# Sixteen weight loads issued from GpSimd's queue instead of SyncE's, in a linear-attention and feed-forward kernel

## The chip, the cores and the metric

One core of a Trainium2 chip runs the whole program. The metric is the device time of one execution in microseconds (us), and the smaller the better. Before the change the median of three runs is 593.93 us (593.01 to 596.69).

The engines are named as in the profile: PE is TensorE (matmuls), PEld its weight loads, DVE is VectorE, ACT is ScalarE, POOL is GpSimd, and SP is SyncE, which computes nothing and here issues transfers. Each engine works through its own instructions in program order and waits where an operand is not ready. A transfer (DMA) is issued by an engine and then carried out by 16 DMA engines, which all issuers share.

## The reference

The input is a linear attention with a decaying complex state, and the result goes through a feed-forward layer. Batch 4, 8 heads, 768 tokens, head size 48; the feed-forward layer goes from 384 to 2048 and back.

```
for t in range(S):                                  # per batch and head
    new_re = ar * S_re - ai * S_im                  # a_t normalised to |a| <= 0.999
    new_im = ar * S_im + ai * S_re
    S_re, S_im = new_re + outer(k_t, v_t), new_im
    y_t = q_t @ S_re
x = y, heads side by side                           # 3072 x 384
h = x @ w_in                                        # 384 x 2048
out = (h * sigmoid(1.702 * h)) @ w_out              # 2048 x 384
```

The two weight matrices are given in 64-bit floating point, everything else in 32-bit.

## The kernel before

The 3072 tokens are cut into 12 units of 256 tokens (`T`), three to a batch element. Each unit u goes through three parts:

- `prepare(u)` loads the decay (`ri`) and the queries and keys (`qk`), computes the running decay magnitude and angle with ACT and DVE (logarithm, exponential and sine tables on ACT; scans on DVE at L582, L598 and L616), and turns the queries and keys by it (L456). POOL writes one-column edges for the scans (L571 and L575, memsets) and makes small copies (L594, L653). Unit 0 is prepared in two halves of 128 tokens so that PE can begin early.
- The turned queries and keys are moved into another layout by `remap`, which copies from SBUF to SBUF in five transfers (L664, L665, L667), once with source `qr` and once with source `qk`. SP issues them. `attend(u)` needs them: PE computes scores (`p_ps`, L702), transposes (`k_ps`, L748), states (`z_ps`, L755) and outputs (`x_ps`, L728).
- `moe(u)` computes the feed-forward layer in eight slices of 256 hidden columns. H is the first matmul (L794, into `h_ps`), then ACT applies Silu (L803 in unit 0, L807 after it), and O is the second (L827, into `o_ps`). Slice i needs the w_in slice A*i* and the w_out slice U*i*. Each H and O has two pieces. Unit 0 runs on whole 32-bit weights, six matmuls to a piece of H and four to a piece of O; the later units run on weights split into a high and a low part.

The sixteen weight slices are loaded once, in the order A0, A1, U0, A2, U1, A3, U2, A4, U3, A5, U4, A6, U5, A7, U6, U7. One load is a 768 KB transfer of 64-bit values into one of four buffers (`raws`), number n into buffer n mod 4. `convert(n)` makes 32-bit values of it: ACT turns the low words in place (L474), and DVE works in three steps (L475, L478, L481), of which the last frees the buffer. So load n can only start once load n - 4 has passed its L481. `split(n)` makes the high part (L494, ACT) and the low part (L499, DVE).

Later in the program SP also issues 48 loads of weights (`raw_w`) and ten of decay values for a check of the value ranges (L849, L872).

The order of all this is not written by hand. Every operation is added to a `Plan` with an engine, an estimated duration, a rank and what it reads and writes. `forward` runs a list scheduler over the operations: each engine starts at the time given for it in `FREE` (POOL at 3.3), takes the ready operation of lowest rank, and a transfer is put on a single line of transfers with estimated costs. `backward` corrects the ranks from the end, `time` rates the result, and the best order of many rounds is emitted; each engine then executes its part in exactly that order, whatever the real times are. A different cost for one kind of operation can therefore change the order of any engine.

The instructions ahead of the plan are emitted first. On POOL these are a few memsets and copies, the last of them the clearing of `qkh` (L397 and L398).

Of the kernel before, what the change touches and what calls it, by code (L numbers as in the profile page):

```python
# [12 lines left out]
I32 = mybir.dt.int32  # L13
# [63 lines left out]

def lag(a, b):
    return LAG if b != "PE" else 0.0 if a == b else LAG_PE


class Plan:
# [31 lines left out]
    def forward(self, rank, stay):  # L114

        ops, after = self.ops, self.after
        left = [len(o[4]) for o in ops]
        ready = [0.0] * len(ops)
        free = dict(FREE)
        wait = {e: [] for e in ENGINES}  # L120
        can = {e: [] for e in ENGINES}
        table, hw, dma, idle = None, 0.0, 0.0, 0.7
        todo, held = self.groups(), None
        clock = Clock()
        kinds, kind = self.kinds, None
        for n, k in enumerate(left):
            if not k:
                heapq.heappush(wait[ops[n][0]], (0.0, n))
        start = [0.0] * len(ops)
        done = 0  # L130
        while done < len(ops):
            best = None
            for e in ENGINES:
                while wait[e] and wait[e][0][0] <= free[e]:
                    n = heapq.heappop(wait[e])[1]
                    heapq.heappush(can[e], (rank[n], n))
                if can[e]:
                    s = free[e]
                elif wait[e]:
                    s = wait[e][0][0]  # L140
                else:
                    continue
                if best is None or s < best[0]:
                    best = (s, e)
            s, e = best
            if not can[e]:
                while wait[e] and wait[e][0][0] <= s:
                    n = heapq.heappop(wait[e])[1]
                    heapq.heappush(can[e], (rank[n], n))
            if e == "ACT":  # L150
                fit = [x for x in can[e] if ops[x[1]][5] in (None, table) or held in (None, ops[x[1]][7])]
                if not fit:
                    later = [free[x] for x in ENGINES if x != e and free[x] > s]
                    later += [wait[e][0][0]] if wait[e] else []
                    if later:
                        free[e] = min(later)
                    else:
                        held = None
                    continue
                pick = min(fit, key=lambda x: x[0] + (SWITCH if ops[x[1]][5] not in (None, table) else 0.0))  # L160
            elif e == "PE":
                pick = min(can[e], key=lambda x: x[0] + (stay if kinds[x[1]] != kind else 0.0))
            else:
                pick = can[e][0]
            n = pick[1]
            dur = ops[n][1]
            hold = [
                r for r, m in wait[e] if r < s + dur - 0.05 and rank[m] < rank[n] - HOLD[e]
                and (e != "ACT" or held in (None, ops[m][7]) or ops[m][5] in (None, table))
            ]  # L170
            if hold:
                free[e] = min(hold)
                continue
            can[e].remove(pick)
            heapq.heapify(can[e])
            if e == "SP":
                free[e] = s + 0.06 + 0.65 * (ops[n][8] - 1)
                hw = max(hw, s + 0.06) + 0.47 * ops[n][8]
                dma = max(dma, hw + 0.6) + dur
                end = dma + 0.9  # L180
            else:
                if ops[n][5] not in (None, table):
                    dur += max(0.0, LOAD - (s - idle))
                    table = ops[n][5]
                if e == "PE":
                    dur += CHANGE if kinds[n] != kind else 0.0
                    kind = kinds[n]
                free[e] = end = clock.end(s, dur, ops[n][8]) if e == "PE" else s + dur
            if e == "ACT":
                idle = end  # L190
                if ops[n][7] is not None:
                    todo[ops[n][7]] -= 1
                    held = ops[n][7] if todo[ops[n][7]] else None
            start[n] = s
            done += 1
            for m in after[n]:
                left[m] -= 1
                ready[m] = max(ready[m], end + lag(e, ops[m][0]))
                if not left[m]:
                    heapq.heappush(wait[ops[m][0]], (ready[m], m))  # L200
        return start, free["PE"]

    def backward(self, when):
# [14 lines left out]
        while done < len(ops):  # L218
            best = None
            for e in ENGINES:  # L220
                while wait[e] and wait[e][0][0] <= free[e]:
                    n = heapq.heappop(wait[e])[1]
                    heapq.heappush(can[e], (-when[n], n))
                if can[e]:
                    s = free[e]
                elif wait[e]:
                    s = wait[e][0][0]
                else:
                    continue
                if best is None or s < best[0]:  # L230
                    best = (s, e)
            s, e = best
            if not can[e]:
                while wait[e] and wait[e][0][0] <= s:
                    n = heapq.heappop(wait[e])[1]
                    heapq.heappush(can[e], (-when[n], n))
            if e == "ACT":
                fit = [x for x in can[e] if ops[x[1]][5] in (None, table) or held in (None, ops[x[1]][7])]
                if not fit:
                    later = [free[x] for x in ENGINES if x != e and free[x] > s]  # L240
                    later += [wait[e][0][0]] if wait[e] else []
                    if later:
                        free[e] = min(later)
                    else:
                        held = None
                    continue
                pick = min(fit, key=lambda x: x[0] + (SWITCH if ops[x[1]][5] not in (None, table) else 0.0))
                can[e].remove(pick)
                heapq.heapify(can[e])
                n = pick[1]  # L250
                if ops[n][7] is not None:
                    todo[ops[n][7]] -= 1
                    held = ops[n][7] if todo[ops[n][7]] else None
            else:
                n = heapq.heappop(can[e])[1]
            dur = ops[n][1]
            if e == "SP":
                free[e] = s + max(dur, 0.47)
                end = s + 0.9 + dur + 1.13
            else:  # L260
                if ops[n][5] not in (None, table):
                    dur += LOAD if table else 0.0
                    table = ops[n][5]
                free[e] = end = s + dur
            late[n] = end
            done += 1
            for m in ops[n][4]:
                left[m] -= 1
                ready[m] = max(ready[m], end + lag(ops[m][0], e))
                if not left[m]:  # L270
                    heapq.heappush(wait[ops[m][0]], (ready[m], m))
        return late

    def time(self, order, load):
# [7 lines left out]
        for n in order:  # L282
            e, dur = ops[n][0], ops[n][1]
            s = max([free[e]] + [ends[d] + lag(ops[d][0], e) for d in ops[n][4]])
            if e == "SP":
                free[e] = s + 0.06 + 0.65 * (ops[n][8] - 1)
                hw = max(hw, s + 0.06) + 0.47 * ops[n][8]
                dma = max(dma, hw + 0.6) + dur
                ends[n] = dma + 0.9
                continue  # L290
            if ops[n][5] not in (None, table):
                dur += max(0.0, load - (s - idle))
                table = ops[n][5]
            if e == "PE":
                dur += CHANGE if kinds[n] != kind else 0.0
                kind = kinds[n]
            free[e] = ends[n] = clock.end(s, dur, ops[n][8]) if e == "PE" else s + dur
            if e == "ACT":
                idle = s + dur
# [38 lines left out]
def attention_moe(ctx: ExitStack, tc: tile.TileContext, qk_in, v, a_in, w_in, w_out, qn, kn, vn, an, bn, out):  # L338
# [119 lines left out]
    def convert(n):  # L458
# [10 lines left out]
        def ti():  # L469
            return weights.whole(m, j).bitcast(I32)  # L470

        add("SP", 2.19, rk - 4, lambda: dma(out=raw.bitcast(I32), in_=(w_in if m == "A" else w_out)[j].bitcast(I32)),
            w=[kg, kl], name=f"f{n}")
        add("ACT", a_t(WC) - 0.1, rk - 1, lambda: act(out=low, in_=ulow, func=AF.Copy, scale=2.0**-29), w=[kl])  # L474
        add("DVE", d_t(WC, 2), rk - 1, lambda: dve.tensor_scalar(  # L475
            out=ti(), in0=top, scalar1=3, scalar2=0x3FFFFFFF, op0=ALU.logical_shift_left, op1=ALU.bitwise_and,
# [691 lines left out]
```

## Time and profile before

| | us |
|---|---|
| median of three runs | 593.93 |
| the profiled execution, its own time | 601.2 |
| its span, first to last instruction | 599.4 |
| PE busy in the span | 556.5 |
| DVE busy | 484.9 |
| ACT busy | 279.6 |
| POOL busy | 26.3 |
| mean granted clock of PE, as a share | 0.994 |

All transfers of the program, 77.52 MB, stand on one queue, that of SP. The sixteen loads take 7.5 us (w_in) and 8.4 us (w_out) in the median from issue to landing.

In a timeline row stand the start, the duration, the engine, the line, the operation, what is written and read, the shape and a count; in brackets the engine's idle time before it and what ended it. "SPq" is the issuing of a transfer by SP, not the transfer. In the chain of waits, "DMA raw<-in_w_in_dram" is a transfer on which something waited, from issue to landing. The table of stages gives for each stretch its length, the busy time of each engine with the number of instructions, the granted clock of PE, the mean busy share of the 16 DMA engines and the rate.

### The profile page before, as it was taken

To read this page: it belongs to the slowest core of one execution; us is meant where nothing else is said; L and a number is where in the kernel's file an instruction comes from. 1 tells how busy PE (TensorE), PEld (TensorE's weight loads), DVE (VectorE), ACT (ScalarE), POOL (GpSimd) and SP (SyncE) were. 2 spreads that over 40 slices of the span, in tenths; PEclk is the share of its full clock that TensorE was granted. 3 is DMA by queue.
4 is the path that set the end of the run, shared out by engine and by line. 5 is a ranking of instruction groups with operands and counts; after the bars stand their busy time and mean duration, and the time that the engine had idled before them with its cause. 6 is when DMAs were issued, how large, how long until landed. Compare 5 with 4: busy or idle time off the path is not lost.

```text
span 599.4 us, 14244 instructions
## 1 busy us (share of the span) xinstructions
PE 556.5 (93%) x5804; PEld 513.8 (86%) x5804; DVE 484.9 (81%) x1003; ACT 279.6 (47%) x468; POOL 26.3 (4%) x75
## 2 busy tenths in 40 slices
PE   0489959999999999999999999999999999999997
PEld 0367637999998999989999989988999989999997
DVE  7999859998968988979979789869979889555543
ACT  7877457546337354354373552552473542211210
POOL 4110001000101000000010000000001000000000
PEclk9999979999999999999999999999999999999999
DMA  8479972272283362374670861772670732732110
GB/s 336 140 253 345 213 180 78 57 153 68 71 187 97 86 160 96 92 157 135 126 208 19 177 198 37 150 223 57 138 201 19 153 129 68 137 86 70 63 45 30
DMA packets 31525, 78.46 MB, mean 131 GB/s; under 512 B 4448, under 2 KB 9568, under 8 KB 31456
## 3 DMA queue, kind: packets, MB, share of 16 engines
q1 hardware_dynamic: 31456, 77.52, 48.3%
q8 instruction: 46, 0.75, 0.5%
q14 instruction: 23, 0.19, 0.1%
HBM read 53.87 MB, written 4.72 MB: 98 GB/s over the span
## 4 chain that ended last, share of the span: by engine, by line
PE 76%; DMA 10%; DVE 8%; ACT 2%; SPq 2%; issue 1%; DVEq 0%; ACTq 0%
PE h_ps L794 30%; PE o_ps L827 30%; PE x_ps L728 6%; PE p_ps L702 5%; DMA raw_w<-in_w_out_dram 4%; DMA raw_w<-in_w_in_dram 3%; PE k_ps L748 2%; PE z_ps L755 2%; DMA raw<-in_w_in_dram 2%; SPq L667 1%; DVE fit L854 1%; DVE s L616 1%; DMA raw<-in_w_out_dram 1%; SPq L664 1%; DVE qk L456 1%
## 5 line engine op out<-in xcount | busy, mean ns | idle before, releaser
L807 ACT ACTIVATE g<-h_ps 128x256 f32<-128x256 f32 x176 | 62.6, 382 | 219.6 <-PE h_ps L794 132.5
L794 PE MATMUL h_ps<-xhi,hiA 128*128 128x256 f32 x528 | 151.6, 287 | 1.6 <-issue 1.1
L794 PE MATMUL h_ps<-xlo,hiA 128*128 128x256 f32 x528 | 149.0, 282 | 0.0
L794 PE MATMUL h_ps<-xhi,loA 128*128 128x256 f32 x528 | 149.0, 282 | 0.0
L794 PEld LDWEIGHTS h_ps<-xhi,hiA 128*128 128x128 f32 x528 | 100.2, 190 | 4.0 <-issue 2.1
L794 PEld LDWEIGHTS h_ps<-xhi,loA 128*128 128x128 f32 x528 | 100.5, 190 | 0.0
L794 PEld LDWEIGHTS h_ps<-xlo,hiA 128*128 128x128 f32 x528 | 100.4, 190 | 0.2
L827 PE MATMUL o_ps<-hiU,gh 128*128 128x384 f32 x352 | 93.9, 346 | 1.4 <-DVE osb L838 1.0
L827 PE MATMUL o_ps<-loU,gh 128*128 128x384 f32 x352 | 89.6, 335 | 0.0
L827 PE MATMUL o_ps<-hiU,gl 128*128 128x384 f32 x352 | 89.6, 335 | 0.0
L810 DVE CAST gh<-g 128x256 fp32r<-128x256 f32 x176 | 48.9, 288 | 39.9 <-ACT g L807 35.6
L812 DVE TENSOR_TENSOR gl<-g,gh 128x256 fp32r<-128x256 f32 x176 | 72.1, 422 | 5.6
L827 PEld LDWEIGHTS o_ps<-loU,gh 128*128 128x128 f32 x352 | 63.7, 188 | 0.0
L827 PEld LDWEIGHTS o_ps<-hiU,gl 128*128 128x128 f32 x352 | 63.6, 188 | 0.0
L827 PEld LDWEIGHTS o_ps<-hiU,gh 128*128 128x128 f32 x352 | 58.2, 189 | 5.6 <-issue 2.0
L854 DVE TENSOR_REDUCE fit<-raw_w 128x1 f32<-128x256 f32 x96 | 38.2, 413 | 25.5 <-DMA raw_w<-in_w_out_dram 16.3
L456 DVE TENSOR_TENSOR qk<-qk,s 128x768 f32<-128x768 f32 (+1 forms) x52 | 46.0, 892 | 0.2
L1005 ACT ACT_TABLE_LOAD x35 | 44.9, 1283 | 1.4 <-PEq L1156 0.8
L702 PEld LDWEIGHTS p_ps<-qkh 128*64 128x64 f32 x768 | 36.4, 136 | 10.4 <-issue 4.5
L702 PE MATMUL p_ps<-qkh 128*64 128x128 f32 (+1 forms) x768 | 42.7, 252 | 2.2 <-DVE pm L706 2.2
L706 DVE TENSOR_TENSOR pm<-p_ps,mask 128x512 f32<-128x512 f32 x48 | 33.0, 688 | 10.8 <-PE p_ps L702 10.5
L728 PE MATMUL x_ps<-pm,v 128*32 128x128 f32 x768 | 38.2, 278 | 1.5 <-DVE pm L706 1.4
(94 smaller groups left out, 753.3 us busy)
## 6 DMA issues: line engine op xcount, KB each, us to landing
v<-in_v_dram SPq DMA_DIRECT2D x24, 352.0 KB, 4.0
ri<-in_a_dram SPq DMA_DIRECT2D x11, 768.0 KB, 5.0
qk<-in_qk_dram SPq DMA_DIRECT2D x11, 768.0 KB, 5.1
qkh<-qr SPq DMA_DIRECT2D x22, 288.6 KB, 5.8
qkh<-qk SPq DMA_DIRECT2D x22, 288.6 KB, 7.3
raw<-in_w_in_dram SPq DMA_DIRECT2D x8, 768.0 KB, 7.5
raw<-in_w_out_dram SPq DMA_DIRECT2D x8, 768.0 KB, 8.4
raw_w<-in_w_in_dram SPq DMA_DIRECT2D x24, 256.0 KB, 2.8
```

The lines of the kernel that those rows point to most:

```text
L456: add(en, t, rank, lambda: e.tensor_tensor(out=out, in0=a, in1=b, op=alu), **kw)
L702: mm(p_ps[to : to + HL, j, lo:L], lhsT=at(h, 1, c)[:, lo : lo + HL], rhs=at(h, 0, c)[:, lo:L], start=True, stop=True)
L706: add("DVE", d_t(CW), rk(4 * c + hh), lambda hh=hh: dve.tensor_tensor(out=pm[hh].rearrange("p (a b) t -> p a b t", b=2), in0=p_ps.rearrang ...
L728: mm(x_ps[32 * j : 32 * j + 32, r, :], lhsT=lt, rhs=rt, start=n == 0, stop=n == len(steps) - 1)
L748: nc.tensor.transpose(k_ps[:, j, 0:KD], at(4 * hh + j, 1, c)[0:KD], ident[0:KD, 0:KD])
L794: mm(h_ps[hb][:, f, :], lhsT=ww[:, r * T + f * P : r * T + (f + 1) * P], rhs=x[:, r, :], start=n == 0, stop=n == last)
L807: add("ACT", a_t(T) - 0.15, rk(i), lambda hb=hb, f=f: act(out=g32[:, f, :], in_=h_ps[hb][:, f, :], func=AF.Silu, scale=SLOPE), r=[f"h{hb}. ...
L810: add("DVE", d_t(T, 2), rk(i), lambda gb=gb, f=f: dve.tensor_copy(out=high.g(gb)[:, f, :], in_=g32[:, f, :]), r=[f"g.{f}"], w=[f"gh{gb}.{f}"])
L812: add("DVE", d_t(T), rk(i), lambda gb=gb, f=f: dve.tensor_tensor(out=glo[gb][:, f, :], in0=g32[:, f, :], in1=high.g(gb)[:, f, :].bitcast(F ...
L827: mm(o_ps[t], lhsT=x[:, f, t * L : (t + 1) * L], rhs=y[:, f * DM : (f + 1) * DM], start=i == 0 and f == 0 and n == 0, stop=i == NP - 1 and ...
L854: add("DVE", d_t(CK), rk + 2, lambda x=x, op=op: dve.tensor_reduce(out=f_w[:, x, n : n + 1], in_=weights.looked_at()[:, :, 1], op=op, axis ...
L1005: nc.scalar.preload_act_table_set(o[5])
```

## The change

The sixteen loads are issued with POOL's `dma_start` instead of SP's. In the plan they become operations of POOL of the kind "dma", and the planner learns what an issue occupies on each engine. Nothing else is changed: the loads' sources, destinations, sizes, buffers and ranks stay, and so does `FREE`.

```diff
+def issue(e, n):
+    return 0.06 + 0.65 * (n - 1) if e == "SP" else (0.65 if e == "ACT" else 1.0) * n
...
-            if e == "SP":
-                free[e] = s + 0.06 + 0.65 * (ops[n][8] - 1)
+            if e == "SP" or kinds[n] == "dma":
+                free[e] = s + issue(e, ops[n][8])
                 hw = max(hw, s + 0.06) + 0.47 * ops[n][8]
                 dma = max(dma, hw + 0.6) + dur
                 end = dma + 0.9
...
-            if e == "SP":
-                free[e] = s + max(dur, 0.47)
+            if e == "SP" or self.kinds[n] == "dma":
+                free[e] = s + max(dur if e == "SP" else 0.0, issue(e, ops[n][8]), 0.47)
                 end = s + 0.9 + dur + 1.13
...
-        add("SP", 2.19, rk - 4, lambda: dma(out=raw.bitcast(I32), in_=(w_in if m == "A" else w_out)[j].bitcast(I32)),
-            w=[kg, kl], name=f"f{n}")
+        add("POOL", 2.19, rk - 4, lambda: pool.dma_start(out=raw.bitcast(I32), in_=(w_in if m == "A" else w_out)[j].bitcast(I32)),
+            w=[kg, kl], name=f"f{n}", kind="dma")
```

The first pair of lines that differ stands in `forward` and, in the same form, in `time`; the second in `backward`; the last in `convert`. For the planner one load occupies POOL for 1.0 us, where it occupied SP for 0.06.

More of the change, by code (lines that the diff above doesn't have):

```diff
@@ L180, in forward @@
                 end = dma + 0.9
+                if e == "ACT":
+                    idle = free[e]
             else:
@@ L189, in forward @@
             if e == "ACT":
-                idle = end
+                idle = free[e]
                 if ops[n][7] is not None:
@@ L284, in time @@
             s = max([free[e]] + [ends[d] + lag(ops[d][0], e) for d in ops[n][4]])
-            if e == "SP":
-                free[e] = s + 0.06 + 0.65 * (ops[n][8] - 1)
+            if e == "SP" or kinds[n] == "dma":
+                free[e] = s + issue(e, ops[n][8])
                 hw = max(hw, s + 0.06) + 0.47 * ops[n][8]
@@ L289, in time @@
                 ends[n] = dma + 0.9
+                if e == "ACT":
+                    idle = free[e]
                 continue
```

## The prediction

> **What bounds the kernel now.** I read the page first, then the busy time by stage, then the timeline of the worst stage, then the queues at the start.
>
> ```profile
> span 599.4 us, 14244 instructions
> PE 556.5 (93%) x5804; PEld 513.8 (86%) x5804; DVE 484.9 (81%) x1003; ACT 279.6 (47%) x468; POOL 26.3 (4%) x75
> ```
>
> TensorE (PE) is busy for 556.5 of 599.4 us, so at most 42.9 us are to be had without touching the arithmetic. The stages show where those lie; the columns are span, then busy time and count on PE, PEld, DVE, ACT and POOL, then granted clock, DMA share, GB/s.
>
> ```profile
> 35.00:60.00 25.00, 22.09 (x223) 17.15 (x224) 24.85 (x38) 19.45 (x29) 1.78 (x5) 1.00 0.87 333
> 60.00:65.00 5.00, 5.00 (x21) 3.65 (x20) 5.00 (x9) 4.06 (x7) 0.00 (x0) 1.00 0.72 228
> 65.00:70.00 5.00, 5.00 (x21) 3.66 (x20) 5.00 (x7) 1.41 (x3) 0.00 (x0) 1.00 1.04 169
> 70.00:75.00 5.00, 4.79 (x19) 3.11 (x17) 3.38 (x5) 1.74 (x4) 0.00 (x0) 1.00 1.04 235
> 75.00:80.00 5.00, 0.00 (x0) 0.00 (x0) 0.19 (x1) 0.13 (x1) 0.00 (x0) 0.79 1.00 151
> 80.00:85.00 5.00, 3.16 (x12) 2.15 (x14) 4.38 (x6) 4.01 (x5) 0.00 (x0) 0.53 0.72 229
> 85.00:100.00 15.00, 15.00 (x212) 10.83 (x207) 13.35 (x20) 11.50 (x16) 0.20 (x2) 1.00 0.36 129
> 100.00:350.00 250.00, 249.13 (x2661) 235.28 (x2662) 216.48 (x441) 123.51 (x203) 9.26 (x30) 1.00 0.48 118
> 350.00:599.40 249.40, 241.08 (x2550) 228.58 (x2544) 181.34 (x417) 84.89 (x159) 5.61 (x18) 1.00 0.40 103
> ```
>
> From 85 us on PE hardly pauses (0.9 us in the 250 us after 100). The 16 loads all lie before that. So the change is decided in the start-up and in one hole: between 75 and 80 us no engine computes, while the DMA engines are full (share 1.00) at only 151 GB/s. The timeline and the chain show the hole:
>
> ```profile
> 62.17 1.18 SPq L664 DMA_DIRECT2D qkh<-qr  x2
> 64.68 0.97 DVE L481 CUSTOM_DVE_ANT_0 valA<-raw,valA 128x1536 uint16<-128x1536 uint16 x1
> 66.71 0.52 SPq L472 DMA_DIRECT2D raw<-in_w_in_dram  x1
> 67.94 3.10 SPq L664 DMA_DIRECT2D qkh<-qk  x2
> 68.62 0.97 DVE L481 CUSTOM_DVE_ANT_0 valU<-raw,valU 128x1536 uint16<-128x1536 uint16 x1
> 72.04 1.46 PE L794 MATMUL h_ps<-x,valA 128*128 128x256 f32 x6
> 74.86 0.98 SPq L472 DMA_DIRECT2D raw<-in_w_out_dram  x2
> 79.81 0.56 DVE L475 TENSOR_SCALAR valA<-raw 128x768 int32<-128x768 int32 x1 [6.32 <-DMA raw<-in_w_in_dram]
> 79.87 0.92 ACT L474 ACTIVATE raw<-raw 128x768 int32<-128x768 uint32 x1 [7.59 <-DMA raw<-in_w_in_dram]
> 81.84 2.93 PE L794 MATMUL h_ps<-x,valA 128*128 128x256 f32 x6 [7.05 <-ACT g L803]
> 84.69 0.89 PE L702 MATMUL p_ps<-qkh 128*64 128x128 f32 x16
> ```
>
> ```profile
> 66.71 13.08 DMA raw<-in_w_in_dram
> ```
>
> Load A7 (the last of w_in) is issued at 66.71, behind the five transfers of remap `qr`, and lands 13.08 us later. ACT and DVE stand in order at A7's conversion; the Silu (L803) that would free `h_ps` stands behind it on ACT, so PE waits 7.05 us, from 74.8. Its next six matmuls take 2.93 us instead of 1.46, at a granted clock of 0.53. The hole costs 7.05 + 1.47 = 8.5 us.
>
> **The change part by part.**
>
> *Issue of the late loads.* A7 uses the buffer that A5 leaves at 64.68 + 0.97 = 65.65; SP issues it 1.06 us after, because the remap occupies SP. U6's buffer is free at 68.62 + 0.97 = 69.59, and U6 leaves at 74.86, 5.3 us late. On POOL these delays go. That is what the change removes; the bytes stay, and so does the DVE work that frees the buffers (DVE is busy 5.00 of 5.00 us in both stages before 70).
>
> *What the hole becomes.* A7 no longer stands behind `qr` in SP's order, so its landing at 79.8 should come forward by several us, and the Silu behind it too. Then the second piece after the hole is late next: scores of unit 1 (L702, 84.69), which need remap `qk`.
>
> ```profile
> L667 SPq DMA_DIRECT2D qkh<-qk x2: 507/530/554, 73.2 to 74.2; - x2
> DMA to landing us min/median/max: 9.0/10.6/13.3
> ```
>
> ```profile
> L472 SPq DMA_DIRECT2D raw<-in_w_out_dram x2: 378/440/503, 74.9 to 75.5; - x2
> DMA to landing us min/median/max: 9.8/10.4/11.1
> ```
>
> Its last transfer lands at 74.2 + 9.0 = 83.2; U7, the last load, at 75.5 + 11.1 = 86.6. The DMA engines are full from 65 to 80, so A7, U6 and U7 can only come earlier at the remap's expense. How a second queue shares with SP's no row here shows. The latest landing of `qk` is that of everything, 86.6. The earliest is that of a remap with nothing beside it, the next unit's:
>
> ```profile
> L702 PE MATMUL p_ps<-qkh x16: 217/246/288, 128.5 to 129.1; 128*64 128x128 f32 x8, 128*64 128x64 f32 x8
> L664 SPq DMA_DIRECT2D qkh<-qk x2: 522/556/591, 120.6 to 121.2; - x2
> ```
>
> There the scores start 128.5 - 120.6 = 7.9 us after the first `qk` transfer; here 67.94 + 7.9 = 75.8. Between 75.8 and 86.6 I take 82.0, near the row of before (83.2), since the same bytes cross the same full engines, and a little earlier since half of what A7 had ahead of it passes. Scores then start at about 82.3 against 84.69: a gain of 2.4 us (bounds: 8.5, when the hole closes, and a loss of 86.6 + 0.3 - 84.69 = 2.2). I assume that PE's new order keeps the scores second after the hole; PE runs H0.6's second half meanwhile at full clock, and then waits.
>
> The Trainium skill (DMA: Bandwidth & Descriptors, section "Queues, rings and completion order") says that each DMA engine takes packets in turn from the queues that have work. By that rule A7 would progress at half pace beside the remap and the remap would lose as much; no run here shows two such queues yet, and by it `qk` would lie near the middle of the bounds, 81.2, a gain of 3.2.
>
> *The four first loads.* They leave SP at 1.7 to 4.7 us now. On POOL they stand behind its opening memsets.
>
> ```profile
> 4.34 3.52 POOL L398 MEMSET qkh<- 128x4104 f32 x1
> 7.80 0.10 POOL L575 MEMSET s<- 128x3 f32 x1
> 10.94 1.05 DVE L582 TENSOR_TENSOR_SCAN s<-s,s 128x129 f32<-128x129 f32 x3
> L472 SPq DMA_DIRECT2D raw<-in_w_in_dram x8: 327/475/648, 1.7 to 66.7; - x8
> ```
>
> POOL is free at 4.34 + 3.52 = 7.86. The planner takes POOL to be free at 3.3 us and the loads have no predecessor, so it will put all four ahead of the edge memsets (L571, L575), which in its model wait for DVE. The memsets, at 7.80 now, then run at 7.86 + 4p, with p the time in which POOL issues one load; the scan L582, at 10.94, needs them. No DMA is issued from POOL here, so p is bounded: below by SP's issue of the same transfer, 0.33 us (no slip then, the memsets are done at 9.2), above by the longest POOL instruction, 3.52 us. I take p = 1.0: near SP's row, which is the same transfer, but above its longest, 0.65, since POOL has issued none here. The memsets end at about 12.0 and unit 0's preparation slips by 12.0 - 10.94 = 1.1 us (bounds: 0, and 7.86 + 14.1 - 10.94 = 11.0). This chain leads over remap 0 to the first real matmuls, so the slip is paid in full. That A0 lands some 4 us later than now costs nothing as long as the planner places its conversion later; if not, ACT and DVE pay up to as much again, inside the upper bound.
>
> *Loads five to eight.* Their buffers are free from 30.3 us, SP issues them only at 35.72, after the remap of unit 0.
>
> ```profile
> L481 DVE CUSTOM_DVE_ANT_0 valA<-raw,valA x3: 952/952/953, 28.5 to 35.9; 128x1536 uint16<-128x1536 uint16 x3
> 35.72 4.34 DMA raw<-in_w_out_dram
> ```
>
> They leave up to 5 us earlier. I cost that at nothing: DVE, which must convert them, is busy 24.85 of the next 25 us, and PE runs without a weight wait until 74.8. If DVE had room it would be worth up to those 5 us.
>
> *Waits that POOL takes on.* Twelve loads wait on POOL for a buffer, and behind them stand edge memsets and small copies of unit 1.
>
> ```profile
> 35.23 0.10 POOL L571 MEMSET s<- 128x3 f32 x1 [5.76 <-ACT s L443]
> 41.16 1.85 DVE L582 TENSOR_TENSOR_SCAN s<-s,s 128x257 f32<-128x257 f32 x3
> 92.89 0.10 POOL L575 MEMSET s<- 128x3 f32 x1 [48.11 <-DVE s L572]
> ```
>
> L571 has 5.9 us before its scan at 41.16; the copies are through at 92.89 - 48.11 = 44.8, some 17 us before the remap at 62.17 that needs them, and then POOL has nothing until 92.89. Cover enough; I cost it at nothing, and without the first cover each further issue ahead of L571 would move the scan by p.
>
> *Sum.* 601.2 us (the profiled execution; its span is 599.4 and 1.8 lie around it) - 2.4 + 1.1 = 599.9. The median of the runs, 593.93, is 7.3 us under the profiled one, so I carry the difference over: 593.93 - 1.3 = 592.6 us.
>
> **The rivals.** A measurement here tells a change of about 1%, 5.9 us, from none.
>
> *B, the hole closes.* A7 and `qk` both land by about 76, or PE's new order has the rest of H0.6, H0.7 and O0.5 (five pieces of about 1.46, 7.3 us) to run before the scores. For it: 65 to 80 us moves 169 to 235 GB/s where 35 to 60 moved 333, so the engines are full but slow, and a second queue may mix better. Against it: the share is already 1.00, and in PE's present order the scores come second. 593.93 - 8.5 + 1.1 = 586.5; without the slip 585.4.
>
> *C, POOL issues slowly (slower than before).* The place is the start, the price 4p - 3.1 us on unit 0's chain. With the gain of 2.4 kept it is slower than before from p = 1.4, and measurably from p = (5.9 + 2.4 + 3.1) / 4 = 2.9; if `qk` lands last as well (+2.2 instead of -2.4), from 1.7. For it: one POOL copy of three elements takes 1.64 us and another 0.19, so something holds POOL up at times while DVE works.
>
> ```profile
> 452.93 1.64 POOL L594 COPY fit<-s 128x3 f32<-128x3 f32 x1 [10.44 <-DVE s L582]
> 190.14 0.19 POOL L594 COPY fit<-s 128x3 f32<-128x3 f32 x1 [2.60 <-DVE s L582]
> ```
>
> Against it: what POOL only writes, such as the memsets L575 and L571, takes 0.10 in the rows above. With p = 2.0 and `qk` last: 593.93 + 4.9 + 2.2 = 601.0. The Trainium skill (SBUF — State Buffer, section "SBUF: two separate sides") has a rule that speaks for C: POOL writes such a transfer's descriptors itself, and DVE instructions in a two-port mode lock it out meanwhile; it gives 620 ns for one transfer alone and 3100 ns beside one such instruction. By it p could reach an estimated 3.1 and the start would slip 9.3 us; no run here shows it yet.
>
> *D, nothing is gained.* The hole belongs to the wait for DMA bytes whichever queue they are on, `qk` lands at 83.2 to 84.4 as before, and the slip remains: 593.93 + 1.1 = 595.0. A hole that only the profiled execution has (its 7.3 us over the median are about the hole's size) gives the same.
>
> **How the numbers follow.** My forecast 0.50, B 0.22, C 0.18, D 0.10. Faster by over 1% is B (0.22) and an early edge of the forecast (0.04): 0.26. Slower by over 1% is C (0.18) and a planner's order that falls badly for A0 (0.04): 0.22. Within 1%: 0.52. The time is the forecast's, 592.6, own range 589 to 596. The range takes in B, to 585.4, and C, to 601.0; beyond lie the highest p and a hole that closes together with a better start.
>
> **What would show it.** L472 on POOL's queue, first at about 7.9 us; L571 and L575 after the fourth, near 12; L582 near 12. A7 issued within 2 us of A5's last conversion and landing before 77; PE's next long wait in 74 to 85 named for `qkh` or L702, not for L803. The forecast is wrong if that wait is gone (B), if p is over 2 us (C), or if PE after 100 us has more than about 3 us of new pauses, which would put the cause in the planner's order and not in the queues.

## The result and the profile after

The changed kernel takes 620.31 us in the median of four runs (618.34 to 622.34). The kernel before, on the same chip, takes 594.26 (593.01 to 596.69). The ratio is 1.0417 [1.0378, 1.0457]: slower by 26 us, and above the range of 585.4 to 601.0. The profiled execution took 620.45 us.

```profile
span 618.8 us, 14262 instructions
PE 559.2 (90%) x5804; PEld 516.5 (83%) x5804; DVE 489.1 (79%) x1003; ACT 280.6 (45%) x468; POOL 42.4 (7%) x91
```

PE does the same work (556.5 us busy before), so most of the 26 us are pauses. POOL's busy time has grown by 16 us, where sixteen issues of a little over half a microsecond make 9. After the diff the lines of the kernel stand eight higher: the load is L480, the copies L661, the memsets L579 and L583, the remap L672 to L675, the scores L710, H L802 and O L835.

The hole of 7.05 us on which the prediction worked belongs to one execution of the kernel before. In another, of 596.12 us (experiment *e0*), it is 1.98 us:

```profile
77.45 1.56 PE L794 MATMUL h_ps<-x,valA 128*128 128x256 f32 x6 [1.98 <-ACT g L803]
```

I compare with that one. Here are the four stages of the changed kernel, then of the kernel before in that execution. The columns are length, busy time and count of PE, PEld, DVE, ACT and POOL, granted clock, DMA share, GB/s.

```profile
0.00:35.00 35.00, 9.99 (x70) 8.38 (x72) 28.66 (x64) 27.30 (x44) 12.74 (x26) 1.00 0.63 216
35.00:60.00 25.00, 18.01 (x229) 14.38 (x226) 19.21 (x29) 14.46 (x22) 2.75 (x7) 0.80 0.80 290
60.00:110.00 50.00, 38.40 (x189) 27.53 (x191) 34.74 (x49) 24.77 (x38) 16.36 (x9) 0.86 0.56 149
110.00:618.80 508.80, 492.84 (x5330) 466.19 (x5321) 406.50 (x864) 214.09 (x367) 10.56 (x49) 1.00 0.44 111
```

```profile
0.00:35.00 35.00, 11.50 (x86) 9.62 (x90) 29.40 (x66) 27.73 (x45) 9.44 (x20) 1.00 0.65 223
35.00:60.00 25.00, 22.24 (x243) 17.06 (x244) 24.96 (x38) 20.67 (x30) 1.80 (x5) 1.00 0.88 319
60.00:110.00 50.00, 47.51 (x427) 36.02 (x426) 46.97 (x72) 34.35 (x52) 2.21 (x5) 1.00 0.56 152
110.00:594.40 484.40, 475.18 (x5056) 451.21 (x5054) 383.25 (x831) 197.61 (x342) 13.17 (x45) 1.00 0.45 114
```

PE's pauses in a stage are its length less PE's busy time. They grow by 25.01 - 23.50 = 1.5 us in the first stage, 6.99 - 2.76 = 4.2 in the second, 11.60 - 2.49 = 9.1 in the third and 15.96 - 9.22 = 6.7 in the last. PE's busy time grows by 559.2 - 556.4 = 2.8. The granted clock of 0.80 and 0.86 in the two stages with long pauses is one reason: after the longest pause four matmuls of O take 2.93 us (101.26), the next four 1.57 (106.40). It need not be the only one, for in *e2* the busy time grows as much (to 559.7) at 0.93 and 1.00. Together 24.3 us; the spans differ by 618.8 - 594.4 = 24.4. So there are four places to explain.

**From 60 to 110 us.** POOL's timeline of the changed kernel:

```profile
71.59 0.53 POOL L480 DMA_DIRECT2D raw<-in_w_in_dram  x1 [1.68 <-DVE valA L489]
72.11 12.80 POOL L661 COPY qr<-fit 128x3 f32<-128x3 f32 x1
84.85 0.53 POOL L480 DMA_DIRECT2D raw<-in_w_out_dram  x1
85.37 0.20 POOL L661 COPY qk<-fit 128x3 f32<-128x3 f32 x1
85.50 0.53 POOL L480 DMA_DIRECT2D raw<-in_w_out_dram  x1
```

A copy of three elements per partition takes 12.80 us. The same copy took 0.19 in the kernel before:

```profile
43.97 0.19 POOL L653 COPY qr<-fit 128x3 f32<-128x3 f32 x1
```

Behind it in POOL's order stand U6 and U7, the last two loads, and SP's remap of unit 1 waits for what it writes. Both leave only when it ends:

```profile
84.93 1.18 SPq L672 DMA_DIRECT2D qkh<-qr  x2
```

```profile
75.00:80.00 5.00, 5.00 (x21) 3.75 (x20) 5.00 (x8) 2.92 (x6) 5.00 (x1) 1.00 0.12 48
80.00:85.00 5.00, 5.00 (x21) 3.64 (x20) 5.00 (x7) 0.49 (x3) 5.00 (x2) 1.00 0.00 0
85.00:100.00 15.00, 4.66 (x19) 3.20 (x17) 2.91 (x5) 5.14 (x6) 1.03 (x3) 0.77 0.95 202
```

The stages show it from the other side. Where the DMA engines of before were busy (share 1.00 from 75 us and 0.72 from 80 in the first profile, 1.02 and 0.99 in *e0*), they now stand idle (0.12, then 0.00), and after 85 us everything crosses at once. PE runs out of work at 89.7 and waits for U6's conversion:

```profile
101.26 2.93 PE L835 MATMUL o_ps<-valU,g 128*128 128x384 f32 x4 [11.60 <-DVE valU L489]
```

U6 itself lands at 93.0. But in DVE's order the first step of U7's conversion comes before the rest of U6's, and the chain of waits goes over U7, issued last of all:

```profile
85.50 12.52 DMA raw<-in_w_out_dram
```

**From 35 to 60 us.** PE waits at 40 us, and DVE ahead of it for a transfer of unit 0's remap:

```profile
45.96 1.55 PE L710 MATMUL p_ps<-qkh 128*64 128x128 f32 x16 [6.11 <-DVE pm L714]
```

```profile
43.81 0.63 DVE L694 TENSOR_TENSOR st<-st,qkh 128x448 f32<-128x448 f32 x1 [5.79 <-DMA qkh<-qk]
```

**After 110 us** there is no single hole, only more pauses of 1 to 1.6 us ahead of the scores. **Before 35 us** the remap of unit 0 starts at 23.16 instead of 21.90.

### The profile page after: what moved, and what is told of

The parts are those of the page before. It is cut to its first block, busy times and chain, and to the rows that moved or that the text cites. A ratio compares the mean times of both kernels' runs of the same rounds, so it can differ in the third digit from the quotient of the medians.

```text
span 618.8 us, 14262 instructions
## 1 busy us (share of the span) xinstructions
PE 559.2 (90%) x5804; PEld 516.5 (83%) x5804; DVE 489.1 (79%) x1003; ACT 280.6 (45%) x468; POOL 42.4 (7%) x91
## 4 chain that ended last, share of the span: by engine, by line
PE 62%; DVE 14%; DMA 13%; SPq 4%; issue 3%; ACT 2%; POOL 1%; DVEq 0%; ACTq 0%; POOLq 0%
PE o_ps L835 25%; PE h_ps L802 24%; PE x_ps L736 5%; DMA raw_w<-in_w_in_dram 4%; PE p_ps L710 4%; DMA raw_w<-in_w_out_dram 4%; DMA raw<-in_w_out_dram 2%; PE k_ps L756 2%; DMA raw<-in_w_in_dram 2%; PE z_ps L763 2%; DVE fit L862 1%; SPq L675 1%; SPq L672 1%; DVE valU L489 1%; SPq L673 1%
## 5 line engine op out<-in xcount | busy, mean ns | idle before, releaser
L802 PE MATMUL h_ps<-xhi,hiA 128*128 128x256 f32 x528 | 151.1, 286 | 2.1 <-ACT g L815 2.1
L802 PE MATMUL h_ps<-xhi,loA 128*128 128x256 f32 x528 | 149.0, 282 | 0.0
L802 PE MATMUL h_ps<-xlo,hiA 128*128 128x256 f32 x528 | 149.0, 282 | 0.0
L802 PEld LDWEIGHTS h_ps<-xhi,hiA 128*128 128x128 f32 x528 | 100.2, 190 | 4.9 <-ACT g L815 3.2
L802 PEld LDWEIGHTS h_ps<-xhi,loA 128*128 128x128 f32 x528 | 100.6, 190 | 0.0
L802 PEld LDWEIGHTS h_ps<-xlo,hiA 128*128 128x128 f32 x528 | 100.4, 190 | 0.2
L835 PE MATMUL o_ps<-hiU,gh 128*128 128x384 f32 x352 | 93.0, 344 | 0.5 <-DVE osb L846 0.5
L835 PE MATMUL o_ps<-loU,gh 128*128 128x384 f32 x352 | 89.7, 335 | 0.0
L835 PE MATMUL o_ps<-hiU,gl 128*128 128x384 f32 x352 | 89.6, 335 | 0.0
L835 PEld LDWEIGHTS o_ps<-loU,gh 128*128 128x128 f32 x352 | 63.7, 188 | 0.0
L835 PEld LDWEIGHTS o_ps<-hiU,gl 128*128 128x128 f32 x352 | 63.6, 188 | 0.0
L835 PEld LDWEIGHTS o_ps<-hiU,gh 128*128 128x128 f32 x352 | 57.9, 190 | 3.3 <-issue 1.4
L710 PEld LDWEIGHTS p_ps<-qkh 128*64 128x64 f32 x768 | 37.8, 140 | 21.2 <-DVE pm L714 13.6
L710 PE MATMUL p_ps<-qkh 128*64 128x64 f32 (+1 forms) x768 | 44.3, 257 | 12.2 <-DVE pm L714 11.5
L464 DVE TENSOR_TENSOR qk<-qk,s 128x768 f32<-128x768 f32 (+1 forms) x52 | 45.5, 889 | 1.5 <-ACT s L650 1.5
L767 ACT ACTIVATE kt<-k_ps 128x448 f32<-128x448 f32 x40 | 21.6, 540 | 41.0 <-PE k_ps L756 21.6
```

The lines of the kernel that those rows point to most:

```text
L464: add(en, t, rank, lambda: e.tensor_tensor(out=out, in0=a, in1=b, op=alu), **kw)
L710: mm(p_ps[to : to + HL, j, lo:L], lhsT=at(h, 1, c)[:, lo : lo + HL], rhs=at(h, 0, c)[:, lo:L], start=True, stop=True)
L767: add("ACT", a_t(4 * KD) - 0.12, rk(4 * c + hh), lambda: act(out=kt[0][:, :, 0:KD], in_=k_ps[:, :, 0:KD], func=AF.Copy), r=["K"], w=["kt"])
L802: mm(h_ps[hb][:, f, :], lhsT=ww[:, r * T + f * P : r * T + (f + 1) * P], rhs=x[:, r, :], start=n == 0, stop=n == last)
L835: mm(o_ps[t], lhsT=x[:, f, t * L : (t + 1) * L], rhs=y[:, f * DM : (f + 1) * DM], start=i == 0 and f == 0 and n == 0, stop=i == NP - 1 and ...
```

## The experiments

My theory after this reading: loads that wait on POOL for a buffer hold the edge copy back until it falls into a stretch in which DVE gives it no access to SBUF, and the copy then holds the remap and the last loads. Its rivals: the planner's new order alone makes the loss; loads five and six, issued from POOL beside the remap, make it; the four first loads make it. Ratios are to the kernel before on the same chip, whose single runs lay between 593 and 603 us.

### The kernel before again (*e0*)

The kernel is unchanged.

> The kernel before, unchanged, for a second profile of it. The first profiled execution took 601.2 us, 7 us over the median of 594, and has a 7.05 us hole on PE at 75 to 82 us. If the hole belongs to every execution, this one shows it too, at 594 or at 601. If it belonged to that one execution, this one takes 593 to 596 and PE has no pause over 2 us between 45 and 100 us; then the change had no hole to close, and its loss against the ordinary execution is 26 us, not 19.

596.12 us, hole 1.98 us (shown above by its stages). The hole's size is that of an execution, not of the kernel.

### Queue alone and order alone (*e1*, *e2*)

*e1* is the kernel before with POOL's issue and the planner still believing in SP; *e2* is the changed kernel, plan and all, with SP issuing. The two edits in this order:

```diff
-        add("SP", 2.19, rk - 4, lambda: dma(out=raw.bitcast(I32), in_=(w_in if m == "A" else w_out)[j].bitcast(I32)),
+        add("SP", 2.19, rk - 4, lambda: pool.dma_start(out=raw.bitcast(I32), in_=(w_in if m == "A" else w_out)[j].bitcast(I32)),
```

```diff
-        add("POOL", 2.19, rk - 4, lambda: pool.dma_start(out=raw.bitcast(I32), in_=(w_in if m == "A" else w_out)[j].bitcast(I32)),
+        add("POOL", 2.19, rk - 4, lambda: dma(out=raw.bitcast(I32), in_=(w_in if m == "A" else w_out)[j].bitcast(I32)),
```

> The order that the planner makes for the kernel before, and only the queue of the 16 loads changed. Theory 1 (the copy): the loads' waits for buffers hold the edge copies L653 of unit 1 behind them on POOL, and a POOL copy that then starts beside an unbroken run of DVE work gets no access until DVE pauses; here four loads more stand ahead of the copy than it had, so it starts near 58 us, ends only when DVE pauses near 73, and remap qr leaves 10 us late: 604 to 615. Theory 2 (the order): the new order of the plan is what costs, so with the old order the time is that of before, 591 to 597. Theory 3 (the bytes): loads five and six, issued early, slow the remap of unit 0 by some 6 us and nothing else matters: 599 to 602.

> The changed kernel's order, with the 16 loads issued from SP again. Theory 1 (the copy): POOL has no waits ahead of the copy, it runs near 57 us in 0.2 to 1 us, remap qr leaves near 73: the hole of 11.6 us is gone or below 3, 600 to 608. Theory 2 (the order): the time stays at 617 to 623. Theory 3 (the bytes): in this order the loads U1 and A3 stand on SP among the transfers of unit 0's remap; if they come ahead of them the remap is later still and the pause near 40 us grows to over 6 us, if behind them it goes: 605 to 625.

*e1*: 610.95 us (610.19 to 611.41), 1.0221 [1.0139, 1.0302]. *e2*: 605.19 (601.84 to 609.81), 1.0124 [1.0022, 1.0226]. Each alone makes the kernel slower. The order costs 0.0124 x 596 = 7 us (by its interval between 1 and 13), so the queue costs some 17 us in the new order and 13 in the old one.

In *e2* the plan is the changed kernel's, and the copy runs where nothing holds it:

```profile
54.34 0.19 POOL L661 COPY qr<-fit 128x3 f32<-128x3 f32 x1
```

So it is the loads ahead of it that move the copy from 54.34 to 72.11. *e2* has no long hole (1.57 us at 82). Its loss lies after 110 us, where PE pauses 16.8 us against 9.2. The waits of PE from 110 to 590 us, in *e2* and then in the kernel before (in total, times, longest):

```profile
PE p_ps L710 <- DVE pm L714: 6.6, 5, 1.8
PE x_ps L736 <- DVE pm L714: 3.9, 3, 1.4
```

```profile
PE p_ps L702 <- DVE pm L706: 1.1, 2, 0.6
PE x_ps L728 <- DVE pm L706: 0.5, 1, 0.5
```

`pm` is DVE's masking of the scores. In the new order PE reaches the following matmuls before DVE has come to it.

In *e1* DVE meets A0's conversion in its old place, and the load lands 4 us later than it did:

```profile
12.90 0.56 DVE L475 TENSOR_SCALAR valA<-raw 128x768 int32<-128x768 int32 x1 [5.08 <-DMA raw<-in_w_in_dram]
```

Unit 0's remap then starts at 26.15, 4.3 us late. The new order has that conversion later, as the prediction supposed, and does not pay these 4 us.

### The edge copies (*e3*, *e4*)

*e3* gives the copies to DVE. *e4* keeps POOL and writes a constant into the same columns in unit 1, so that the instruction reads nothing from SBUF. The two edits in this order:

```diff
-                add("POOL", 0.13, rk(f"rot{x}"), lambda dst=dst: pool.tensor_copy(out=dst[:, :, 2 * n], in_=f_a[:, u, :]),
+                add("POOL", 0.13, rk(f"rot{x}"), lambda dst=dst: dve.tensor_copy(out=dst[:, :, 2 * n], in_=f_a[:, u, :]),
```

```diff
-                add("POOL", 0.13, rk(f"rot{x}"), lambda dst=dst: pool.tensor_copy(out=dst[:, :, 2 * n], in_=f_a[:, u, :]),
+                add("POOL", 0.13, rk(f"rot{x}"), lambda dst=dst: pool.memset(dst[:, :, 2 * n], 1.0) if u == 1 else pool.tensor_copy(out=dst[:, :, 2 * n], in_=f_a[:, u, :]),
```

> The changed kernel with the 24 edge copies L661 executed by DVE at their places in the same order, loads on POOL as in the change. Theory 1 (the copy): each takes below 0.2 us on DVE, remap qr of unit 1 leaves near 73 us instead of 84.9 and U6 near 73 instead of 84.9; the pause of 11.6 us at 90 to 101 shrinks below 4, and the time falls by 8 to 13 us to 607 to 612. Theory 2 (the order) and theory 3 (the bytes): nothing hangs on the copy, 617 to 623.

> The changed kernel with the two edge copies of unit 1 on POOL replaced by memsets of the same three columns, on POOL, at the same places; the decay at the end of unit 1 is left out of the result by that. If what POOL lacks beside DVE is reading (theory 1a), the memset takes 0.1 to 0.5 us, remap qr of unit 1 leaves near 73 instead of 84.9, and the pause of 11.6 us shrinks to about 5 as with the copies on DVE: span 608 to 614. If any access of POOL is held up beside a full DVE (theory 1b), the memset takes over 5 us and the span stays at 616 to 621.

*e3*: 616.89 us, 1.0358 [1.026, 1.0455]. *e4*, one run: 616.5. POOL's timeline of *e4*, and PE's hole in it:

```profile
71.52 0.12 POOL L661 MEMSET qr<- 128x3 f32 x1
74.95 0.53 POOL L480 DMA_DIRECT2D raw<-in_w_out_dram  x1 [3.31 <-DVE valU L489]
```

```profile
93.03 2.93 PE L835 MATMUL o_ps<-valU,g 128*128 128x384 f32 x4 [4.50 <-DVE valU L489]
```

At the same place in POOL's order the instruction that reads nothing takes 0.12 us instead of 12.80. U6 leaves at 74.95 instead of 84.85, and the hole shrinks from 11.60 to 4.50 us (*e3*: 4.64). The pause at 40 us stays in both (5.27 and 5.70). But of the 7 us only some 4 reach the end, less than expected, and *e3*'s interval overlaps that of the changed kernel: the shorter hole is clear, the shorter run is not. By the stages of *e4*, its pauses after 110 us have grown by 2.0 us, and PE's busy time by 1.7: part of the gain is given back later.

### Loads five and six (*e5*), and both cures (*e6*)

*e5* issues U1 and A3 from SP, behind the last transfer of unit 0's remap; the rest stays on POOL. *e6* is *e5* with *e3*'s copies.

```diff
-        add("POOL", 2.19, rk - 4, lambda: pool.dma_start(out=raw.bitcast(I32), in_=(w_in if m == "A" else w_out)[j].bitcast(I32)),
+        add("POOL", 2.19, rk - 4, lambda: (dma if n in (4, 5) else pool.dma_start)(out=raw.bitcast(I32), in_=(w_in if m == "A" else w_out)[j].bitcast(I32)),
...
+    names = [plan.ops[x][6] for x in order]
+    last = max(names.index(f"remap0.{i}.{x}") for i in range(2) for x in range(2))
+    for f in ("f4", "f5"):
+        at = [plan.ops[x][6] for x in order].index(f)
+        if at < last:
+            moved = order.pop(at)
+            order.insert(last, moved)
...
```

> The changed kernel with loads five and six (U1, A3) issued from SP, where they stand behind the last transfer of unit 0's remap; the other 14 loads on POOL. Theory 3 (the bytes): the last transfers of that remap land in about 3 us instead of 8, near 38 instead of 43.5, the pause of 6.1 us at 40 to 46 falls to about 2 as with all loads on SP, and the time falls by 3 to 5 us to 614 to 617. If the pause is the order's or the copy's, it stays and so does the time, 618 to 622.

> The changed kernel with both: the edge copies on DVE and U1, A3 on SP behind the remap. If the copy and the bytes are all that the queue does, what stays is the order's own cost, and the time is that of the order alone: 603 to 609 (605.2 there). If another cost of POOL's queue is left (its issue, its slower landing), it is over 611.

*e5*: 617.28 us (615.19 to 620.46), 1.0352 [1.0276, 1.0428]. The remap's last transfers in the changed kernel, then in *e5* (from issue to landing, shortest, median, longest of four):

```profile
L675 SPq DMA_DIRECT2D qkh<-qk x2: 607/692/776, 35.1 to 35.7; - x2
DMA to landing us min/median/max: 1.9/5.1/8.3
```

```profile
L675 SPq DMA_DIRECT2D qkh<-qk x2: 589/594/599, 34.3 to 35.0; - x2
DMA to landing us min/median/max: 1.9/2.8/3.7
```

With two weight loads issued just before (33.30 and 34.20), a transfer of 16 KB, issued after 35 us, lands up to 8.3 us later; with both issued behind it, 3.7 at most. PE's pause at 40 us falls from 6.11 to 1.98. The copy still takes 12.80 us in *e5* (66.61 to 79.41), and the hole 13.23: the two costs are separate. The run as a whole is 3 us shorter than the changed kernel's, which the two intervals do not tell apart.

*e6*: 611.29 us (608.13 to 615.63), 1.0247 [1.0165, 1.0329]. The two cures together bring back 0.017 x 596 = 10 us of the queue's 17, and less than expected. This interval lies clear of the changed kernel's, [1.0378, 1.0457]. Against the profile of *e2*, PE's pauses are still 2.6 us longer between 60 and 110 us, where the hole is 4.59 instead of 1.57, and 1.8 longer after 110. The chain of *e6* shows U7 in the hole:

```profile
73.06 11.09 DMA raw<-in_w_out_dram
```

U6 and U7 leave at 70.45 and 73.06 now instead of 84.85 and 85.50, beside the remap's `qk` transfers (73.73 to 85.49 us), and take 8.0 and 11.1 us.

### Only the late loads (*e7*)

This is the prediction's gain by itself: the kernel before, with A7, U6 and U7 alone on POOL, where no copy of unit 1 stands behind them.

```diff
-        add("SP", 2.19, rk - 4, lambda: dma(out=raw.bitcast(I32), in_=(w_in if m == "A" else w_out)[j].bitcast(I32)),
+        add("SP", 2.19, rk - 4, lambda: (pool.dma_start if n >= 13 else dma)(out=raw.bitcast(I32), in_=(w_in if m == "A" else w_out)[j].bitcast(I32)),
```

> The kernel before, in its order, with only the last three loads A7, U6, U7 on POOL, whose queue is empty there from 46 to 90 us. As forecast for the change: A7 no longer stands behind remap qr and lands by 76; if the hole at 75 (2 us in the second profile, 7 in the first) then closes, the time is 590 to 593 and the runs of 599 to 601 are gone. Rival: the remap qk of unit 1 loses what the loads win, PE waits for its scores, and the time stays at 593 to 597 or the pause moves to L702 and grows to 598 to 602.

598.37 us (595.49 to 603.8, twelve runs), 1.0028 [0.9992, 1.0064]: no gain. In the chain of its profile, which is of the slowest of the twelve, A7 is no longer behind the remap on SP. It is issued 0.6 us earlier, its buffer being free only at 65.5:

```profile
66.12 14.09 DMA raw<-in_w_in_dram
```

```profile
82.25 2.93 PE L794 MATMUL h_ps<-x,valA 128*128 128x256 f32 x6 [7.67 <-ACT g L803]
```

It lands at 80.21, as in the first profile of before (66.71 + 13.08 = 79.79), and the hole is 7.67 us. A queue of its own does not bring it forward there. U6 and U7 leave almost 5 us earlier (from 70.02 on instead of 74.86), and the three transfers take 13.1 to 14.4 us instead of 9.8 to 13.1. What moves A7 is the time of the transfer itself. In *e0* SP issues it later, at 68.02, and it lands 7.4 us after; in the changed kernel, where the remap had not left yet, it takes 5.4 (71.59 to 77.0). Why the two executions of the same kernel differ by 5.7 us there stays open.

### What lets the copy through (*e8*)

One DVE memset of one column is put behind U5's conversion in the changed kernel. I meant it to run near 75 us.

```diff
-        add("DVE", d_t(WC), rk - 0.5, lambda: dve.tensor_tensor(out=ti(), in0=ti(), in1=low, op=ALU.add), r=[kl], w=[f"v{c}"])
+        def third():
+            dve.tensor_tensor(out=ti(), in0=ti(), in1=low, op=ALU.add)
+            if n == 12:
+                dve.memset(good, 0.0)
+
+        add("DVE", d_t(WC), rk - 0.5, third, r=[kl], w=[f"v{c}"])
```

> The changed kernel with one DVE memset of one column added in the unbroken run of DVE work, right after the last conversion step of U5 (near 75 us). Theory 1a, sharpened: the POOL copy, which reads SBUF, waits not for a long pause of DVE but for one instruction that does not read two operands from SBUF or run at the double rate; then it ends at that memset, about 3 us after its start instead of 12.8, remap qr leaves near 76, the pause of 11.6 us falls to about 6, and the time to 612 to 617. If the copy needs a real pause of DVE, it ends near 85 as before and the time stays at 618 to 622.

619.7 us (615.3 to 625.32), 1.0386 [1.0305, 1.0467]: no difference from the changed kernel. U5's third step runs at 80.72 and not near 75, so the hole shrinks only to 8.74 us. But the copy answers the question. POOL's row, and then DVE's timeline of *e8*:

```profile
71.52 10.19 POOL L666 COPY qr<-fit 128x3 f32<-128x3 f32 x1
```

```profile
77.18 0.94 DVE L464 TENSOR_TENSOR qk<-qk,s 128x768 f32<-128x768 f32 x1
78.05 0.54 DVE L483 TENSOR_SCALAR valU<-raw 128x768 int32<-128x768 int32 x1
78.51 0.54 DVE L483 TENSOR_SCALAR valA<-raw 128x768 int32<-128x768 int32 x1
78.98 0.94 DVE L486 SCALAR_TENSOR_TENSOR valU<-raw,valU 128x768 int32<-128x768 int32 x1
80.72 0.94 DVE L490 CUSTOM_DVE_ANT_0 valU<-raw,valU 128x1536 uint16<-128x1536 uint16 x1
81.60 0.94 DVE L486 SCALAR_TENSOR_TENSOR valA<-raw,valA 128x768 int32<-128x768 int32 x1
81.61 0.06 DVE L492 MEMSET small<- 128x1 f32 x1
```

The copy ends at 71.52 + 10.19 = 81.71, 0.10 us after the memset begins. In the changed kernel it ends at 84.91, 0.13 us after the first DVE instruction that takes an operand from PSUM:

```profile
83.91 0.95 DVE L489 CUSTOM_DVE_ANT_0 valA<-raw,valA 128x1536 uint16<-128x1536 uint16 x1
84.78 0.61 DVE L772 TENSOR_TENSOR st<-z_ps,st 128x448 f32<-128x448 f32 x1
```

Before that DVE ran one instruction after another, either with two inputs in SBUF (L464, L486, L489) or the one-input conversion L483, which does 768 elements in 0.54 us where the others take 0.94. Neither kind let the copy through. The same holds for other copies: the one of 3.52 us in *e2* (L602, at 50.77) ends 0.15 us after the start of a 128x3 TENSOR_SCALAR.

### The order of before with the cures (*e9*), other plans (*e10*, *e11*)

*e9*: kernel before, first six loads on SP, the rest on POOL, copies on DVE. *e10*: kernel before, all loads on SP, but the planner takes SP to be occupied 0.33 us by an issue, as measured, instead of 0.06; only the order changes. *e11*: the changed kernel with the constants that its own profile shows. The three edits in this order; that of *e10* is made in two places:

```diff
-        add("SP", 2.19, rk - 4, lambda: dma(out=raw.bitcast(I32), in_=(w_in if m == "A" else w_out)[j].bitcast(I32)),
+        add("SP", 2.19, rk - 4, lambda: (pool.dma_start if n >= 6 else dma)(out=raw.bitcast(I32), in_=(w_in if m == "A" else w_out)[j].bitcast(I32)),
...
-                add("POOL", 0.13, rk(f"rot{x}"), lambda dst=dst: pool.tensor_copy(out=dst[:, :, 2 * n], in_=f_a[:, u, :]),
+                add("POOL", 0.13, rk(f"rot{x}"), lambda dst=dst: dve.tensor_copy(out=dst[:, :, 2 * n], in_=f_a[:, u, :]),
```

```diff
-                free[e] = s + 0.06 + 0.65 * (ops[n][8] - 1)
+                free[e] = s + 0.33 + 0.65 * (ops[n][8] - 1)
```

```diff
-    return 0.06 + 0.65 * (n - 1) if e == "SP" else (0.65 if e == "ACT" else 1.0) * n
+    return 0.06 + 0.65 * (n - 1) if e == "SP" else (0.65 if e == "ACT" else 0.53) * n
...
-FREE = {"PE": 0.7, "ACT": 0.7, "DVE": 3.6, "POOL": 3.3, "SP": 0.7}
+FREE = {"PE": 0.7, "ACT": 0.7, "DVE": 3.6, "POOL": 7.9, "SP": 0.7}
```

> The order of the kernel before; loads seven to sixteen on POOL, the first six on SP as before, and the edge copies on DVE. If the late first loads, the two loads beside unit 0's remap and the copy are all that the queue costs in that order (611 with all of it), the time is that of before, 593 to 602. If POOL's queue has a further cost, such as the later landing of U6 and U7 beside remap qk, it is over 603.

> The kernel before, all loads on SP, with one constant of the planner changed: the time that one issue occupies SP, 0.33 (the shortest measured) instead of 0.06. Nothing but the order can change. If the extra 8 us of the changed kernel's order after 100 us are the lot of nearly any new order, this one too takes 600 to 610, and PE pauses more after 110 us; if that order was bad for a reason of its own, this one stays at 593 to 600.

> The changed kernel with the planner told what the trace shows of POOL: free at 7.9 us instead of 3.3, and 0.53 us for one issue instead of 1.0. The planner still knows nothing of the copy that gets no access and of loads that slow a remap. Theories 1 and 3: copies stand behind loads again and loads five and six go beside the remap, so both pauses stay and the time is 610 to 625. If wrong constants of the plan were the cause, 594 to 606.

*e9*: 598.93 us (597.45 to 600.81, ten runs), 1.0038 [1.0006, 1.007]. With the start, unit 0's remap and the copies out of the way, the queue's cost in the old order falls from 13 us to 2; and nothing is gained.

*e10*: 592.68 us (592.11 to 594.51, ten runs), 0.9942 [0.9905, 0.9979]. It is the fastest of all kernels here, on SP's queue, by a change of order alone. So another order moves the time by some microseconds, down here and up in *e2*.

*e11*: 608.89 us (607.67 to 610.07), 1.0235 [1.019, 1.028]. A plan with these constants brings back 11 of the 26 us, a little more than expected: the copy now takes 5.42 us and no pause near 90 us exceeds 1.61. The waits for unit 0's remap stay (2.07 and 2.18 us).

## Why the prediction was wrong

**"Waits that POOL takes on": "Cover enough; I cost it at nothing."** This is the step whose failure the runs show best. It took the time of the copies, "through at 92.89 - 48.11 = 44.8", from the profile of before, where nothing stood ahead of them on POOL. In the changed kernel loads that wait for buffers stand ahead, and the copy begins at 72.11. That alone would have cost nothing: the remap has to wait until 73.03 for the rotation on DVE. The price came from the duration, 12.80 us instead of 0.19. Its condition, a DVE without a gap, stood in stages that the prediction quoted: busy 5.00 of 5.00 us. Full cover on DVE was counted as a reason why other things cost nothing, and it is what shut POOL out. *e3* and *e4* show the price, 7 us of the hole, and *e8* what ends the copy. How many of the 7 us reach the end is less sharply measured (about 4).

**Rival C** had the right clue and put it on the wrong instruction. It saw that a POOL copy of three elements once took 1.64 us, "so something holds POOL up at times while DVE works", and priced the issue of the loads with it. Its own row shows what *e8* shows: that copy ends at 452.93 + 1.64 = 454.57, 0.13 us after the start (454.44) of a DVE instruction with an operand in PSUM, L740 on `x_ps`.

The four first issues of the changed kernel were hardly held:

```profile
7.81 1.19 POOL L480 DMA_DIRECT2D raw<-in_w_in_dram  x2
8.99 0.53 POOL L480 DMA_DIRECT2D raw<-in_w_out_dram  x1
10.03 0.12 POOL L583 MEMSET s<- 128x3 f32 x1
```

Here p is 0.53 to 0.6 us instead of 1.0, and not the 2.0 of rival C; the memsets are through at 10.2, and the scan starts at 10.55, earlier than in the profile of before. The term "+1.1" was thus wrong in its working. The remap of unit 0 starts 1.3 us late all the same, after a wait of DVE for ACT (in *e5*, with the same four loads on POOL, at 22.40); no run took that apart.

Later issues were held at times, but briefly. Two of the other twelve take longer, 0.91 and 0.76 us, and both end 0.12 to 0.13 us after a one-input conversion L483 that began while they ran:

```profile
33.30 0.91 POOL L480 DMA_DIRECT2D raw<-in_w_out_dram  x1 [4.45 <-ACT kt L767]
```

```profile
33.52 0.56 DVE L483 TENSOR_SCALAR valU<-raw 128x768 int32<-128x768 int32 x1
```

Beside DVE's two-input instructions an issue takes 0.53 (71.59, beside L464).

The Trainium skill (SBUF — State Buffer, section "Who interferes with whom") separates the two: a DVE instruction with two SBUF inputs shuts out a GpSimd instruction that reads SBUF, and not one that only writes it; it adds, as an inference, that writing descriptors needs the write side. The runs agree: 12.80 us for the copy, 0.12 for a memset in its place, 0.53 for an issue beside a two-input instruction. The copy waited out a whole run of some fifteen DVE instructions, not one. The prediction drew the descriptor rule from that page and passed over this one.

**"Loads five to eight": "They leave up to 5 us earlier. I cost that at nothing."** Wrong by 4 us of PE's pause at 40 us. The cover named there, a busy DVE and a PE without weight waits, protects against a load that is late. The cost was in what an early load takes from the remap beside it (*e5*: pause 1.98 instead of 6.11 us).

**"What the hole becomes": a gain of 2.4 us.** There was none. A7 was held up by what crossed the DMA engines beside it and not by SP's order (*e7*, *e0*); rival B falls with it. One sign nearly came out, by luck: A7 landed at 77.0 ("before 77"), not because it had passed the remap but because the remap was still waiting for the copy. And the hole was sized from one execution, 7.05 us, where another has 1.98; the prediction had named this under D. Its caution, "A7, U6 and U7 can only come earlier at the remap's expense", points the right way: in *e7* they left earlier and took longer.

**The order** had no term in the sum, only a chance of 0.04 and a test: more than about 3 us of new pauses after 100 us "would put the cause in the planner's order". The pauses after 110 us grew by 6.7 us, and *e2* has as much without the queue (7.6). "From 85 us on PE hardly pauses" was read from the 250 us after 100 alone; the last row of the same table has 249.40 - 241.08 = 8.3 us of pauses. PE's waits sit at DVE's masking of the scores; why this order is worse there stays open. *e11* shows that constants nearer the trace help, *e10* that the old ones weren't the best either.

**The sum** was -1.3 us. Measured: about 7 for the order; some 10 for copies and loads five and six together (*e2*, *e6*); the remaining 7 no run takes apart, and these are differences of medians that are each uncertain by some 5. Late loads beside the remap, the start and the lowered clock may have a part in them.

## What to carry to other kernels

A transfer that waits for a buffer makes its issuing engine wait, so before moving it, list every later instruction of that engine, when it will run instead, and beside what. A neighbour that is busy throughout is cover only for work that it does not shut out, as DVE did the copy here. And take no hole from one profile before a second one shows it.

## What the hardware did that I had not expected

- A POOL copy of three elements per partition waited as long as DVE ran two-input instructions from SBUF and one-input conversions (L483) back to back: 12.80 us twice, 10.19 and 5.42. It ended 0.10 to 0.16 us after the start of DVE's first instruction of another kind, a memset, a 128x3 TENSOR_SCALAR or one with an operand in PSUM. Once a gap sufficed: a copy of 9.02 us in *e1* ended at 80.86, when DVE paused for 0.03 us between two of them.
- The issue of a load from POOL takes 0.53 us beside two-input instructions of DVE. Where a one-input conversion of 0.54 to 0.57 us began in the first 0.24 us of the issue, it took 0.76 to 0.92 and ended 0.11 to 0.13 us after the conversion: 14 issues in nine profiles. One such issue in *e6* took 1.23 us.
- A transfer of 16 KB on SP's queue took up to 8.3 us instead of 3.7 while two loads of 768 KB ran from POOL's.
- After a pause of 11.60 us the granted clock was 0.67 in the next ten (100 to 110 us); the four matmuls of O after it took 2.93 us, where eight had taken 2.74 before it.
